# Attention and two expert layers on one core: the projections of q and k as plain f32 in two 64-row halves, and the last tokens as one tile

## The chip, the cores and the metric

The kernel runs on one core of one Trainium2 chip. The metric is the device time of one launch in microseconds (us), as the median of three runs. Two executions agree within 0.2%, about 1.7 us here.

## What is computed

Three stages follow each other. The first is an attention with random features, the second a dense layer with a leaky rectifier, the third a layer of 8 experts of which each token uses one. The change touches the first stage alone.

```python
# B=4 batches, H=8 heads, S=576 tokens, D=64; omega: (M=128, 64)
def phi(x):                                   # x: (B, H, S, 64), scaled by 64**-0.25
    h = einsum('bhsd,md->bhsm', x, omega) - sum(x*x)/2
    return exp(h - max(h)) / sqrt(128)
q_p, k_p = phi(q_s), phi(k_s)
kv = einsum('bhsm,bhsd->bhmd', k_p, v);  z = sum(k_p, tokens)
x  = (q_p @ kv) / (q_p @ z + 1e-6)            # -> (2304, 512)
h  = x @ w_in;  x2 = max(0.01*h, h) @ w_out   # w_in (512, 2048), w_out (2048, 512)
...                                           # 8 experts, top 1, on x2
```

## The kernel before

Heads are worked in 16 **pairs** (two heads of one batch, 128 columns together). Of a head's 576 tokens, 512 are four blocks of 128 and the **last 64** are kept apart: those of both heads of a pair, for q and for k, form one tile "m". Per pair the steps are, by their names in the table `STEPS`: loads `Lk Lq Lm Lv`; squares, halving and sums `s a r` (sums of x*x); transposes on TensorE `Tk Tq Tm` (L520); copies of the transposed tile to SBUF as a high part `xh` and a low part `xl` (L314, L323), both f32r; projections `Pk0 Pk1 Pq0 Pq1 Pm` (L541 to L543), each 128-token block by three matmuls of 256 columns (high by high, high by low, low by high) against a block-diagonal `om_hi` and `om_lo`, so that one matmul gives two token blocks of a head (for "m", q and k); maxima `m` (L551); biases `b c` (L564, or L571 and L572 on GpSimd); exponentials `e` on ScalarE (L583); `KVm KV0 KV1` (L590, L595), plain f32 matmuls of q's and k's features; transposes `F0 F1 Fm` of q's features (L614, L610) and their copies `fc`; numerators `U0 U1` (L629, L634); denominators `dn` (L650 to L654); ratios `xs0 xs1` (L661, L668), where the last tokens are scaled head by head in two instructions of 64 rows; transposes `XT Xm` (L674, L678); and the copies into the dense layer's input `xb` as high and low parts, `yh yl` and, again head by head for the last tokens, `yhm ylm`.

Beside the pairs run two other streams in the same stretch. Ten **conversions** (`RW C0 C1 CX C2 CH CL`, L396 to L421) make f32r high and low parts of the dense weights. And **dense steps** of the first group of 5 weight chunks (45 steps of 256 tokens by one chunk): `M1` (12 matmuls, L750 to L752), `HS GG GH GL` on ScalarE, VectorE and GpSimd, `M2` (6 matmuls of 512 columns in two banks, L791 to L793, 3 for each 128 tokens). A dense step can begin when its tokens' pairs are through `yl` and `ylm`, so 4 pairs of a batch at least.

The order of all these steps on every engine is made before the launch by `issue_order` (L152). It takes the durations of `STEPS` (L52) for each engine on which a step may run ("P" TensorE, "V" VectorE, "A" ScalarE, "G" GpSimd, "D" the DMA queue), ranks written into the table, and the 8 PSUM banks ("+tk" takes a bank, "-tk" gives it back), and puts down step, engine and banks. The kernel issues the steps in that order; an engine works strictly in it. What dense steps are left when the last pair is through (L1361) runs behind it, then the groups of 3 and 8 chunks, then the experts.

Of the kernel before, what the change touches and what calls it, by code (L numbers as in the profile page):

```python
# [9 lines left out]
F32 = mybir.dt.float32  # L10
# [57 lines left out]
    "xlk": ("p", (("V", 0.6, 291.1),), "-tk", "xhk"),  # L68
    "Tm": ("p", (("P", 0.11, -1226.3),), "+tm", "Lm"),
    "xhm": ("p", (("A", 0.158, -513.9), ("V", 0.2, 157.5)), "", "Tm Pm-1"),  # L70
    "xlm": ("p", (("V", 0.2, -1168.8),), "-tm", "xhm"),
    "Tq": ("p", (("P", 0.44, -203.4),), "+tq", "Lq"),
    "xhq": ("p", (("A", 0.47, 1466.0), ("V", 0.6, 259.7)), "", "Tq Pq0-1 Pq1-1"),
    "xlq": ("p", (("V", 0.6, -1992.3),), "-tq", "xhq"),
# [1512 lines left out]
```

## Time and profile before

| | us |
|---|---|
| median of 3 runs (872.69 to 873.39) | 873.34 |
| profiled execution, its own time | 875.46 |
| its span in the trace | 873.4 |
| PE busy / DVE busy in the span | 812.6 / 564.1 |

The span is one execution on the hardware. A PE matmul is pipelined: its row's length holds the way through the array, so matmuls overlap in the rows, and what one costs is the distance to the next one's start. An f32 matmul that is no transpose stands in the trace as two instructions, so the four matmuls of one `KV` step are 8 rows.

### The profile page before, as it was taken

Reading aid. Unit: us, or ns where it says so; the run is one execution under the profiler, and the core shown is the slowest. Engines: PE = TensorE matmul, PEld = TensorE weight load, DVE = VectorE, ACT = ScalarE, POOL = GpSimd, SP = SyncE. Lnnn points to the kernel's source line nnn. Section 1 sums busy time; section 2 is a strip of 40 time slices with the busy share of each in tenths; the row PEclk is TensorE's granted clock in tenths of the full one; section 3 lists DMA queues with packets and bytes.
Section 4 is the critical chain, followed back from the end, with each engine's and each line's share of the span. In section 5 each row is a group of like instructions: output and inputs, shape, how many; then the busy total and the mean of one; then the engine's idle time right before and its main releaser. Section 6 shows DMA issues by size and latency. Waiting matters only on the chain. (4 is left out here: it accounts for less than half of the span.)

```text
span 873.4 us, 14417 instructions
## 1 busy us (share of the span) xinstructions
PE 812.6 (93%) x5018; PEld 727.9 (83%) x5018; DVE 564.1 (65%) x1406; ACT 354.4 (41%) x898; POOL 293.4 (34%) x384
## 2 busy tenths in 40 slices
PE   8988898999999999999999999898888799999993
PEld 8877788899998899999998988786677689987892
DVE  7999999688755627625487988979888222222121
ACT  6776656266536534423333332444432111112110
POOL 6323435121004435424424244444655211111000
PEclk9999979999999999999999999989999899999997
DMA  6433423122117415645112331467561211111100
GB/s 183 125 99 88 125 68 91 49 58 52 39 36 234 142 53 180 228 157 175 44 61 36 50 38 36 110 181 120 98 76 59 62 38 50 50 49 38 36 25 29
DMA packets 68309, 75.73 MB, mean 87 GB/s; under 512 B 32691, under 2 KB 49148, under 8 KB 68094
## 3 DMA queue, kind: packets, MB, share of 16 engines
q1 hardware_dynamic: 64766, 65.19, 28.6%
q0 software_dynamic: 3456, 9.49, 3.5%
q8 instruction: 42, 0.69, 0.4%
q14 instruction: 45, 0.37, 0.2%
HBM read 55.65 MB, written 19.00 MB: 85 GB/s over the span
## 5 line engine op out<-in xcount | busy, mean ns | idle before, releaser
L323 POOL TENSOR_TENSOR glo<-gg,ghi 128x384 fp32r<-128x384 f32 (+1 forms) x93 | 97.6, 1050 | 213.6 <-ACT ghi L314 179.8
L750 PE MATMUL ph<-xb,ring 128*128 128x384 f32 (+1 forms) x444 | 141.4, 319 | 1.3 <-ACT hs L314 0.6
L752 PE MATMUL ph<-xb,ring 128*128 128x384 f32 (+1 forms) x444 | 141.0, 318 | 0.0
L751 PE MATMUL ph<-xb,ring 128*128 128x384 f32 (+1 forms) x444 | 140.3, 316 | 0.0
L760 DVE SCALAR_TENSOR_TENSOR gg<-hs 128x384 f32<-128x384 f32 (+1 forms) x111 | 67.9, 612 | 84.8 <-ACT hs L314 79.7
L925 DVE CUSTOM_DVE_ANT_0 jv<-xl,en 128x512 bf16<-128x512 f32 x144 | 121.2, 865 | 1.4
L791 PE MATMUL px<-ring,ghi 128*128 128x512 f32 x288 | 114.7, 398 | 5.8 <-ACT ghi L314 5.8
L793 PE MATMUL px<-ring,glo 128*128 128x512 f32 x288 | 113.1, 398 | 2.4 <-POOL glo L323 2.4
L792 PE MATMUL px<-ring,ghi 128*128 128x512 f32 x288 | 114.2, 396 | 0.6 <-DVE ring L323 0.6
L750 PEld LDWEIGHTS ph<-xb,ring 128*128 128x128 f32 x444 | 84.4, 190 | 7.1 <-ACT hs L314 1.4
L314 ACT CAST ghi<-gg 128x384 fp32r<-128x384 f32 (+1 forms) x93 | 44.8, 482 | 109.9 <-DVE gg L760 109.8
L751 PEld LDWEIGHTS ph<-xb,ring 128*128 128x128 f32 x444 | 84.4, 190 | 4.0
L752 PEld LDWEIGHTS ph<-xb,ring 128*128 128x128 f32 x444 | 84.5, 190 | 0.3
L314 ACT COPY hs<-ph 128x384 f32<-128x384 f32 (+1 forms) x109 | 47.3, 434 | 86.5 <-PE ph L752 84.4
L1203 DVE SCALAR_TENSOR_TENSOR fh<-fh,fh 128x256 fp32r<-128x256 f32 x48 | 20.4, 425 | 91.0 <-ACT fh L1202 91.0
L793 PEld LDWEIGHTS px<-ring,glo 128*128 128x128 f32 x288 | 54.0, 189 | 16.6 <-POOL glo L323 5.1
L791 PEld LDWEIGHTS px<-ring,ghi 128*128 128x128 f32 x288 | 54.7, 190 | 14.9 <-ACT ghi L314 7.0
L1202 ACT ACTIVATE fh<-fh 128x256 fp32r<-128x256 f32 x48 | 18.5, 386 | 112.7 <-PE fh L1196 112.6
L792 PEld LDWEIGHTS px<-ring,ghi 128*128 128x128 f32 x288 | 54.6, 190 | 9.0 <-DVE ring L323 0.9
L1269 POOL DMA_INDIRECT out_dram<-ot,xg x14 | 14.1, 1008 | 123.6 <-DVE ot L1268 79.4
L1194 PE MATMUL fh<-xth,w 128*128 128x256 f32 x128 | 35.8, 282 | 0.0
L1195 PE MATMUL fh<-xth,w 128*128 128x256 f32 x128 | 35.8, 281 | 0.0
(1272 smaller groups left out, 1958.3 us busy)
## 6 DMA issues: line engine op xcount, KB each, us to landing
xl<-xpart SPq DMA_DIRECT2D x36, 256.0 KB
rawi<-in_moe_w_in_dram SPq DMA_DIRECT2D x16, 512.0 KB
rawo<-in_moe_w_out_dram SPq DMA_DIRECT2D x16, 512.0 KB
rws<-in_moe_w_dram SPq DMA_DIRECT2D x16, 512.0 KB
xpart<-xo SPq DMA_DIRECT2D x18, 256.0 KB
xpart<-xl SPq DMA_DIRECT2D x18, 256.0 KB
xs<-xl SPq DMA_DIRECT2D x18, 256.0 KB
k<-in_k_dram SPq DMA_DIRECT2D x16, 256.0 KB
```

Source lines behind the costliest of these rows:

```text
L314: (A.copy if e == "A" else ENG[e].tensor_copy)(out_, in_)
L323: eng.tensor_tensor(lo, src, hi.bitcast(F32), op=ALU.subtract)
L750: PE.matmul(ph, wh, xb[blk][:, 0, kk, d], start=(kk == 0), stop=False)
L751: PE.matmul(ph, wl, xb[blk][:, 0, kk, d], start=False, stop=False)
L752: PE.matmul(ph, wh, xb[blk][:, 1, kk, d], start=False, stop=(kk == 3))
L760: V.scalar_tensor_tensor(gs["gg"], gs["hs"], 0.01, gs["hs"], op0=ALU.mult, op1=ALU.max)
L791: PE.matmul(px, ghi[:, d], r[:, 2, :], start=first, stop=False)
L792: PE.matmul(px, ghi[:, d], r[:, 3, :], start=False, stop=False)
L793: PE.matmul(px, glo[:, d], r[:, 2, :], start=False, stop=last)
L925: V.tensor_tensor_reduce(out=jv, in0=xfin[t], in1=rt["en"][:, e, :], scale=1.0, scalar=0.0, op0=ALU.mult, op1=ALU.add, accum_out=lg[:, j, ...
L1194: PE.matmul(ph, wh, xh, start=(kk == 0), stop=False)
L1195: PE.matmul(ph, wl, xh, start=False, stop=False)
```

## The change

The projections of the 512-token part take plain f32 operands. The copy of the transposed tile is one step, `xk xq xm` (L314 in the changed kernel's helper), with no low part. `Pk` and `Pq` are one step each, of 8 matmuls: for each of the 4 blocks of the transposed tile, whose rows 0 to 63 are an even token block of a head and rows 64 to 127 the odd one, one matmul with the upper and one with the lower 64 rows, each against its half of `om_bd`, into two different banks ("++pk" takes two). `Pm` is one f32 matmul of 256 columns. What stood by head in `KV`, `U`, `mk0/mk1` and `xs` now stands by token parity. The denominators are 10 columns wide: the last tokens of both heads are added, inverted and masked together (`own`), scaled by one instruction into `xm`, and moved by an ordinary f32 matmul against `two` (the sum of both halves of the identity) to 128 rows by 64 columns, so that `yhm` and `ylm` are one instruction each instead of two.

```diff
-    "xhk": ("p", (("A", 0.47, -769.1), ("V", 0.6, 1084.7)), "", "Tk Pk0-1 Pk1-1"),
-    "xlk": ("p", (("V", 0.6, 291.1),), "-tk", "xhk"),
-    "Pk0": ("p", (("P", 0.69, -189.8),), "+pk0", "xlk"),
+    "xk": ("p", (("A", 0.47, 462.5), ("V", 0.6, -718.0)), "-tk", "Tk Pk-2"),
+    "Pk": ("p", (("P", 1.4, -292.1),), "++pk", "xk"),
...
-                late = t + dur if x == e and e != "D" else end + 0.15 * (e == "V" and x == "G")
+                late = t + dur if x == e == "P" else end + 0.15 * (e == "V" and x == "G")
...
-            PE.matmul(o, hi, om_hi, start=True, stop=False)
-            PE.matmul(o, hi, om_lo, start=False, stop=False)
-            PE.matmul(o, lo, om_hi, start=False, stop=True)
+        ps = [bank(f"pj{i}{x}{j}") for j in range(2)]
+        xT = st[i].pop("x" + x)
+        for u in range(4):
+            for j in range(2):
+                r = slice(j * D, (j + 1) * D)
+                PE.matmul(
+                    ps[j][:, u * M : (u + 1) * M], xT[r, u * P : (u + 1) * P],
+                    om_bd[r, j * M : (j + 1) * M], start=True, stop=True,
+                )
+    def proj_last(i):
+        ps = st[i]["pm"] = bank(f"pj{i}m")
+        PE.matmul(ps[:, 0 : 2 * M], st[i].pop("xm"), om_bd, start=True, stop=True)
...
-        for h in range(2):
-            r, _, d = m_view(i, h)
-            V.tensor_scalar_add(dn[r, 8:9], d, 1e-6)
+        V.tensor_scalar_add(dn[:, 0:4], u_view(i, 0)[:, :, D], 1e-6)
+        V.tensor_scalar_add(dn[:, 4:10], u_view(i, 1)[:, :, D], 1e-6)
         V.reciprocal(dn, dn)
+        V.tensor_tensor(dn[:, 8:10], dn[:, 8:10], own, op=ALU.mult)
...
-            for j in range(2):
-                r, u, _ = m_view(i, j)
-                V.tensor_scalar_mul(xms[i % 2][r, j * D : (j + 1) * D], u, dn[r, 8:9])
+            V.tensor_tensor(
+                xms[i % 2].rearrange("p (h d) -> p h d", h=2), u_view(i, 1)[:, 4:6, 0:D],
+                dn[:, 8:10].unsqueeze(2).to_broadcast([P, 2, D]), op=ALU.mult,
+            )
...
-        PE.transpose(ps[:, 0:P], xms[i % 2], ident)
+        PE.matmul(ps[:, 0:D], xms[i % 2], two, start=True, stop=True)
```

The table's ranks are all new, so the whole order of the first stretch is new. On VectorE, before, from the denominators of pair 2 (`dn`) to the copies of its last tokens (`xpm` to `xb`):

```order
L650 TENSOR_SCALAR dn_136<-u_0_841 128x4
L650 TENSOR_SCALAR dn_136<-u_1_853 128x4
L653 TENSOR_SCALAR dn_136<-u_1_853 64x1 x2
L654 RECIPROCAL dn_136<-dn_136 128x9
L661 TENSOR_TENSOR xt_910<-u_0_841,dn_136 128x4x64
L314 COPY qT_919<-pq_887 128x512
L661 TENSOR_TENSOR xt_910<-u_1_853,dn_136 128x4x64
L668 TENSOR_SCALAR xm_138<-u_1_853,dn_136 64x64 x2
L323 TENSOR_TENSOR xl4q<-tr4q,xh4q 128x512
L323 TENSOR_TENSOR xl4m<-tr4m,xh4m 128x128
L314 CAST xb_131<-xpm_942 64x64 x2
L323 TENSOR_TENSOR xb_131<-xpm_942,xb_131 64x64 x2
```

Now, the same place (pair 2 again):

```order
L652 TENSOR_SCALAR dn_132<-u_0_743 128x4
L653 TENSOR_SCALAR dn_132<-u_1_790 128x6
L654 RECIPROCAL dn_132<-dn_132 128x10
L655 TENSOR_TENSOR dn_132<-dn_132,own 128x2
L320 TENSOR_TENSOR xb_127<-xpm_807,xb_127 128x64
L662 TENSOR_TENSOR xt_832<-u_0_743,dn_132 128x2x2x64
L662 TENSOR_TENSOR xt_832<-u_1_790,dn_132 128x2x2x64
L669 TENSOR_TENSOR xm_134<-u_1_790,dn_132 128x128
L566 SCALAR_TENSOR_TENSOR mx4k_788<-ss_728,mx4k_788 128x4x2
L509 TENSOR_REDUCE ss_728<-sqs4m 128x2
L549 TENSOR_REDUCE mx4m<-pj4m 128x2
L509 TENSOR_REDUCE ss_728<-sqs4q 128x8
```

The ratios of the last tokens (`xm`) are one row of 128 columns where they were two of 64 rows, their low part in `xb` is one row where it was two, a mask row has come to the denominators, and no low parts `xl4q` and `xl4m` follow. On TensorE, before, the last-token projection of pair 4 with the work around it (`pq` is the transpose of q's features, `xp` and `xpm` that of the ratios, `tr` that of the inputs, `kv` the `KV` steps):

```order
L614 MATMUL pq_935<-ident,f3q_902 128x128 x4
L678 MATMUL xpm_942<-ident,xm_138 128x128
L674 MATMUL xp_944<-ident,xt_910 128x128 x4
L520 MATMUL tr5k<-ident,k_711 128x128 x4
L541 MATMUL pj4m<-om_hi,xh4m 128x256
L542 MATMUL pj4m<-om_lo,xh4m 128x256
L543 MATMUL pj4m<-om_hi,xl4m 128x256
L590 MATMUL kv_973<-v1s_135,f3m 128x130
L595 MATMUL kv_973<-v1s_135,f3k_801 128x65 x4
L595 MATMUL kv_973<-v1s_135,f3k_825 128x65 x4
L541 MATMUL pj4q_994<-om_hi,xh4q 128x256
```

Now, around the last-token projection of pair 6:

```order
L532 MATMUL pj6k_1089<-om_bd,x6k 128x128
L532 MATMUL pj6k_1090<-om_bd,x6k 128x128
L594 MATMUL kv_1118<-v1s_131,f5m 128x130
L601 MATMUL kv_1118<-v1s_131,f5k_1021 128x65 x4
L678 MATMUL xp_1137<-ident,xt_1120 128x128 x4
L516 MATMUL tr6m<-ident,m_979 128x128
L682 MATMUL xpm_1149<-two,xm_135 128x64
L620 MATMUL pq_1154<-ident,f4q_1128 128x128 x4
L516 MATMUL tr6q<-ident,q_1005 128x128 x4
L542 MATMUL pj6m<-om_bd,x6m 128x256
L620 MATMUL pq_1180<-ident,f4q_1113 128x128 x4
```

The three projection rows of a last-token tile are one, the projections of a pair stand in one block of 8 with the two banks in turn, and the last tokens' ratios go through a matmul against `two`. On TensorE the projections of q and k stand in 28 such blocks between other work, for 32 steps. Further on in TensorE's order, 4 `M1` steps stand ahead of `XT` of pair 8 before, and 14 now; ahead of `XT` of pair 15 it is 22 and 25.

## Rows read from the trace of the kernel before

**Rows 1.** The page: span, busy time, busy tenths of DVE in 40 slices

```profile
span 873.4 us, 14417 instructions
...
PE 812.6 (93%) x5018; PEld 727.9 (83%) x5018; DVE 564.1 (65%) x1406; ACT 354.4 (41%) x898; POOL 293.4 (34%) x384
...
DVE  7999999688755627625487988979888222222121
```

**Rows 2.** Stretches: length, busy PE, PEld, DVE, ACT, POOL (count), PE clock, DMA

```profile
0.00:150.00 150.00, 133.13 (x980) 119.76 (x981) 139.19 (x377) 99.80 (x302) 60.63 (x144) 0.95 0.40 111
120.00:130.00 10.00, 8.37 (x44) 7.38 (x44) 9.26 (x28) 5.72 (x18) 3.81 (x6) 0.66 0.32 92
150.00:256.00 106.00, 104.35 (x808) 98.85 (x809) 80.07 (x241) 55.54 (x168) 15.60 (x23) 1.00 0.16 44
256.00:873.00 617.00, 575.11 (x3233) 509.29 (x3231) 344.82 (x791) 199.03 (x430) 217.14 (x217) 0.98 0.34 88
```

**Rows 3.** PE in order of time: start, length, line, operation, out<-in, form, count

```profile
149.56 0.28 PE L543 MATMUL pj10q<-om_hi,xl10q 128*128 128x256 f32 x1
149.89 0.39 PE L750 MATMUL ph<-xb,ring 128*128 128x256 f32 x1
...
254.86 0.27 PE L678 MATMUL xpm<-ident,xm 128*128 128x128 f32 x1
254.97 0.60 PE L674 MATMUL xp<-ident,xt 128*128 128x128 f32 x4
...
256.10 0.40 PE L791 MATMUL px<-ring,ghi 128*128 128x512 f32 x1
256.34 0.39 PE L792 MATMUL px<-ring,ghi 128*128 128x512 f32 x1
```

**Rows 4.** DVE in order of time, behind the turn; last: idle and releaser

```profile
161.12 0.43 DVE L760 SCALAR_TENSOR_TENSOR gg<-hs 128x256 f32<-128x256 f32 x1 [0.85 <-ACT hs L314]
```

**Rows 5.** PE in order of time: f32 halves, then a projection of pair 5

```profile
65.57 1.90 PE L595 MATMUL kv<-v1s,f4k 128*128 128x65 f32 x16
67.28 0.36 PE L541 MATMUL pj5q<-om_hi,xh5q 128*128 128x256 f32 x1
67.48 0.28 PE L542 MATMUL pj5q<-om_lo,xh5q 128*128 128x256 f32 x1
67.59 0.28 PE L543 MATMUL pj5q<-om_hi,xl5q 128*128 128x256 f32 x1
```

**Rows 6.** DVE in order of time: the steps that the change touches

```profile
62.79 0.57 DVE L668 TENSOR_SCALAR xm<-u,dn 64x64 f32<-64x64 f32 x2
63.40 0.29 DVE L323 TENSOR_TENSOR xl5m<-tr5m,xh5m 128x128 fp32r<-128x128 f32 x1
63.60 0.68 DVE L551 TENSOR_REDUCE mx5k<-pj5k 128x4 f32<-128x512 f32 x1
64.20 0.47 DVE L314 CAST xb<-xpm 64x64 fp32r<-64x64 f32 x2
64.70 0.48 DVE L323 TENSOR_TENSOR xb<-xpm,xb 64x64 fp32r<-64x64 f32 x2
65.20 0.69 DVE L323 TENSOR_TENSOR xl5q<-tr5q,xh5q 128x512 fp32r<-128x512 f32 x1
65.81 0.41 DVE L551 TENSOR_REDUCE mx5m<-pj5m 128x2 f32<-128x256 f32 x1
```

**Rows 7.** DVE in order of time: one conversion twice, and denominators

```profile
46.91 0.41 DVE L396 TENSOR_SCALAR tti<-rawi 128x512 int32<-128x512 int32 x1
...
138.78 0.95 DVE L396 TENSOR_SCALAR tti<-rawi 128x512 int32<-128x512 int32 x1
...
140.38 0.22 DVE L650 TENSOR_SCALAR dn<-u 128x4 f32<-128x4 f32 x2
...
141.12 0.76 DVE L661 TENSOR_TENSOR xt<-u,dn 128x256 f32<-128x256 f32 x2
```

**Rows 8.** One line (the numerators): weight loads, min, median and max ns

```profile
L629 PEld LDWEIGHTS u<-kvf,qT x256: 186/192/245, 20.5 to 250.4; 128*128 128x128 f32 x128
```

More of the change, by code (lines that the diff above doesn't have):

```diff
@@ L170, in issue_order @@
             if name[0] == "P":
-                need.add(("ol", 0))
+                need.add(("oh", 0))
             if name == "M1":
@@ L208, in issue_order @@
         spots = {}
-        for b, among in (("+h", (0, 1)), ("+x", (2, 3, 4, 5, 6)), ("+", range(8))):
-            n = 2 if b == "+x" else 1
+        for b, among in (("+h", (0, 1)), ("+x", (2, 3, 4, 5, 6)), ("+", range(8)), ("++", range(8))):
+            n = 2 if b in ("+x", "++") else 1
             got = sorted((rooms[r] + 0.05, r) for r in among if r in rooms)[:n]
@@ L230, in issue_order @@
         if kind_of_room(s):
-            t = max(t, spots.get(b, spots["+"])[0])
-            got = spots[b][1] if b in spots else (
-                max(r for r in rooms if rooms[r] + 0.05 <= t),)
+            t = max(t, spot(b)[0])
+            got = spots[b][1] if b in spots else tuple(
+                sorted(r for r in rooms if rooms[r] + 0.05 <= t)[-len(spot(b)[1]) :])
             for r in got:
                 del rooms[r]
-            held[b[1:], i] = list(got)
+            held[b.lstrip("+"), i] = list(got)
         for x, _, _ in modes:
@@ L253, in issue_order @@
         if b[:1] == "-":
-            rooms[held[b[1:], i - NRING + 1 if b == "-x" else i][name == "XV"]] = end
+            rooms[held[b[1:], i - NRING + 1 if b == "-x" else i][name in ("XV", "ek1", "eq1")]] = end
         for u in users.get(s, ()):
             for x in AHEAD:
-                late = t + dur if x == e and e != "D" else end + 0.15 * (e == "V" and x == "G")
+                late = t + dur if x == e == "P" else end + 0.15 * (e == "V" and x == "G")
                 ready[u][x] = max(ready[u][x], late)
@@ L339, in tile_attention_moe_moe, with om_step @@
         PE.matmul(warm[:, 0:P], wz, wz, start=True, stop=True)
-    om_hi = atp.tile([P, 2 * M], F32R, name="om_hi", tag="om_hi")
-    om_lo = atp.tile([P, 2 * M], F32R, name="om_lo", tag="om_lo")
-    obd = atp.tile([P, 2 * M], F32, name="obd", tag="xt", bufs=2)
-    V.memset(obd, 0.0)
-    A.copy(om_hi, obd)
-    V.tensor_copy(om_lo, obd)
+    om_bd = atp.tile([P, 2 * M], F32, name="om_bd", tag="om_bd")
+    V.memset(om_bd, 0.0)
     oms = {}
-    def om_step(name):
+    def om_step(name, e):
         if name == "om":
@@ L435, in tile_attention_moe_moe @@
     v1s = [atp.tile([P, 5, 2, D + 2], F32, name=f"v1s{j}", tag=f"v1{j}") for j in range(2)]
-    dns = [atp.tile([P, 9], F32, name=f"dn{j}", tag=f"dn{j}") for j in range(2)]
+    dns = [atp.tile([P, 10], F32, name=f"dn{j}", tag=f"dn{j}") for j in range(2)]
     xms = [atp.tile([P, P], F32, name=f"xm{j}", tag=f"xm{j}") for j in range(2)]
@@ L443, in tile_attention_moe_moe @@
             G.memset(v1s[j][h * 64 : h * 64 + 64, 4, h, D : D + 1], 1.0)
-        G.memset(xms[j], 0.0)
+    own = atp.tile([P, 2], F32, name="own", tag="own")
+    G.memset(own, 0.0)
+    for h in range(2):
+        G.memset(own[h * 64 : h * 64 + 64, h : h + 1], 1.0)
+    two = atp.tile([P, D], F32, name="two", tag="two")
+    G.tensor_tensor(two, ident[:, 0:D], ident[:, D:P], op=ALU.add)
     def part(i):
@@ L521, in trans, with trans_copy, proj @@
         st[i]["t" + p] = ps[:, :w]
-    def trans_hi(i, e, p):
-        ps = st[i]["t" + p]
-        st[i]["xh" + p] = hi = atp.tile([P, ps.shape[1]], F32R, name=f"xh{i}{p}", tag=f"xh{p}")
-        copy(e, hi, ps)
-    def trans_lo(i, p):
-        ps = st[i].pop("t" + p)
-        st[i]["xl" + p] = lo = atp.tile([P, ps.shape[1]], F32R, name=f"xl{i}{p}", tag=f"xl{p}")
-        split_lo(V, lo, ps, st[i]["xh" + p])
-    def proj(i, p):
-        x, n, u0 = (p[0], 2, 2 * int(p[1]) * P) if p != "m" else ("m", 1, 0)
-        ps = bank(f"pj{i}{p}")
-        for j in range(n):
-            u = slice(u0 + j * P, u0 + (j + 1) * P)
-            hi, lo = st[i]["xh" + x][:, u], st[i]["xl" + x][:, u]
-            o = ps[:, j * 256 : (j + 1) * 256]
-            PE.matmul(o, hi, om_hi, start=True, stop=False)
-            PE.matmul(o, hi, om_lo, start=False, stop=False)
-            PE.matmul(o, lo, om_hi, start=False, stop=True)
-        st[i]["p" + p] = ps
+    def trans_copy(i, e, p):
+        ps = st[i].pop("t" + p)
+        st[i]["x" + p] = x = atp.tile([P, ps.shape[1]], F32, name=f"x{i}{p}", tag=f"x{p}", bufs=2)
+        copy(e, x, ps)
+    def proj(i, x):
+        ps = [bank(f"pj{i}{x}{j}") for j in range(2)]
[7 more added lines that the diff above has]
+                )
+        for j in range(2):
+            st[i][f"p{x}{j}"] = ps[j]
+    def proj_last(i):
+        ps = st[i]["pm"] = bank(f"pj{i}m")
+        PE.matmul(ps[:, 0 : 2 * M], st[i].pop("xm"), om_bd, start=True, stop=True)
     def largest(i, p):
@@ L562, in bias @@
         mx = st[i]["b" + x][:, : 2 * (r.stop - r.start)]
+        if x != "m":
+            mx = mx.rearrange("p (b h a) -> p h a b", b=2, h=2)
+            sv = sv.rearrange("p (h a b) -> p h a b", h=2, b=2)
         if e == "V":
@@ L570, in bias @@
             t = t[:, : 2 * (r.stop - r.start)]
+            if x != "m":
+                t = t.rearrange("p (h a b) -> p h a b", h=2, b=2)
             G.tensor_scalar_mul(t, sv, half)
@@ L590, in kv_last, with kv @@
         PE.matmul(pk, st[i]["fm"][:, 1, :], vs[i][:, 4, :, 0 : D + 1], start=True, stop=False)
-    def kv(i, h):
-        f = st[i].pop(f"fk{h}")
-        for t in range(4):
-            PE.matmul(
-                st[i]["kv"][:, h, :], f[:, t, :], vs[i][:, t, h, 0 : D + 1],
-                start=False, stop=(t == 3 and "kv_" in st[i]),
-            )
-        st[i]["kv_"] = h
+    def kv(i, j):
+        f = st[i].pop(f"fk{j}")
+        for h in range(2):
+            for a in range(2):
+                PE.matmul(
+                    st[i]["kv"][:, h, :], f[:, 2 * h + a, :], vs[i][:, 2 * a + j, h, 0 : D + 1],
+                    start=False, stop=(h == 1 and a == 1 and "kv_" in st[i]),
+                )
+        st[i]["kv_"] = j
     def kv_copy(i, e):
@@ L621, in f_copy, with numer @@
         copy(e, t, ps[:, 0:w])
-    def numer(i, h):
-        ps = st[i][f"u{h}"] = bank(f"u{i}_{h}")
-        qT, kvf = st[i].pop(f"qT{h}"), st[i]["kvf"]
-        for t in range(4):
+    def numer(i, j):
+        ps = st[i][f"u{j}"] = bank(f"u{i}_{j}")
+        qT, kvf = st[i].pop(f"qT{j}"), st[i]["kvf"]
+        for g in range(4):
             PE.matmul(
-                ps[:, t * (D + 1) : (t + 1) * (D + 1)], qT[:, t * P : (t + 1) * P],
-                kvf[:, h, :], start=True, stop=True,
+                ps[:, g * (D + 1) : (g + 1) * (D + 1)], qT[:, g * P : (g + 1) * P],
+                kvf[:, g // 2, :], start=True, stop=True,
             )
-        if h == 1:
+        if j == 1:
             PE.matmul(
@@ L637, in numer, with u_view, ratio @@
             )
-    def u_view(i, h):
-        return st[i][f"u{h}"][:, 0 : 4 * (D + 1)].rearrange("p (t d) -> p t d", t=4)
-    def m_view(i, h):
-        r, c = slice(h * 64, h * 64 + 64), (4 + h) * (D + 1)
-        return r, st[i]["u1"][r, c : c + D], st[i]["u1"][r, c + D : c + D + 1]
+    def u_view(i, j):
+        w = 6 if j else 4
+        return st[i][f"u{j}"][:, 0 : w * (D + 1)].rearrange("p (g d) -> p g d", g=w)
     def dens(i):
         dn = dns[i % 2]
-        for h in range(2):
-            V.tensor_scalar_add(dn[:, 4 * h : 4 * h + 4], u_view(i, h)[:, :, D], 1e-6)
-        for h in range(2):
-            r, _, d = m_view(i, h)
-            V.tensor_scalar_add(dn[r, 8:9], d, 1e-6)
+        V.tensor_scalar_add(dn[:, 0:4], u_view(i, 0)[:, :, D], 1e-6)
+        V.tensor_scalar_add(dn[:, 4:10], u_view(i, 1)[:, :, D], 1e-6)
         V.reciprocal(dn, dn)
-    def ratio(i, h):
+        V.tensor_tensor(dn[:, 8:10], dn[:, 8:10], own, op=ALU.mult)
+    def ratio(i, j):
         if "xt" not in st[i]:
@@ L688, in x_parts @@
             w = min(XB - off, end - t0)
-            if m:
-                for h in range(2):
-                    r = slice(h * 64, h * 64 + 64)
-                    yield st[i]["xpm"][r, h * 64 : h * 64 + 64], [
-                        xb[blk][r, j, hp, off : off + w] for j in range(2)
-                    ]
-            else:
-                yield st[i]["xp"][:, t0 - b * S : t0 - b * S + w], [
-                    xb[blk][:, j, hp, off : off + w] for j in range(2)
-                ]
+            at = 0 if m else t0 - b * S
+            yield st[i]["xpm" if m else "xp"][:, at : at + w], [
+                xb[blk][:, j, hp, off : off + w] for j in range(2)
+            ]
             t0 += w
@@ L1328, in tile_attention_moe_moe @@
             if kind == "o":
[L1329 removed]
+                om_step(name, e)
             elif kind == "p":
```

34 lines of the change are left out of this document (15 added, 19 removed), and 153 rows, old and new, of the table STEPS.

## Prediction

> **What bounds the kernel now.** I read the page first, then stretches of the span, then the two engines in order of time. On the page PE is busy for 93% of the span, DVE for 65%, and the tenths of DVE are high only at the front and in the routing far behind [rows 1]. The stretches split the change's part in two [rows 2]. From 0 to 150 us DVE is busy for 139.2 of 150 us, PE at a mean clock of 0.95; from 120 to 130 us PE starts only 44 matmuls and the clock is 0.66. From 150 to 256 us PE is busy for 104.4 of 106 us at full clock, and DVE falls to 80.1. So DVE ends last in the first part and PE in the second. The turn is seen in time: a projection of pair 10 starts at 149.56, and at 149.89 a run of dense steps begins [rows 3], after which DVE's dense work waits for ScalarE and so for PE [rows 4]. The last pair's transposes are at 254.86 and 254.97 [rows 3]. What follows, 617 us, is the same work in both kernels, except that it begins with as many dense steps fewer as the first stretch took in.
>
> PE's busy share hides what it lost, since a row holds the way through the array: a dense matmul of 256 columns is 0.28 long and the next starts 0.12 later, a 512-column one 0.23 later, and one f32 half-instruction of the `KV` step costs (67.28 - 65.57)/16 = 0.107 [rows 3, 5]. The 980 matmuls up to 150 us [rows 2], less 35 for warming up, come to 114 us at such distances (0.12 on the mean). **PE lost about 35.5 us before 149.9 and nearly nothing from there to 256.** That is all that a lighter DVE can win.
>
> How the 35.5 come about can be counted from the order. I added, step by step, what DVE and PE are handed, with durations from distances of starts in the trace. DVE's sum runs ahead of PE's by at most 29.4 us, 144.3 against 115.0, just where the run of dense steps begins. With 6.1 us of start-up that is the 35.5. The count and the trace agree, so I use the same count for the changed order.
>
> **The change, part by part.** *DVE.* A pair loses the low parts of q, k and m: 0.61 + 0.61 + 0.20 (65.20 to 65.81, 63.40 to 63.60 [rows 6]), 1.42 us. The last tokens' ratios go from two rows (62.79 to 63.40, 0.61) to one, about 0.30; their low part from 0.50 (64.70 to 65.20) to 0.22, and their high part likewise where DVE has it, 11 pairs before and 8 after [rows 6]. The denominators go from five rows in 0.74 us (140.38 to 141.12) [rows 7] to four that depend on each other; I keep 0.74. Over 16 pairs this takes off 16 x (1.42 + 0.31 + 0.28) + 11 x 0.50 - 8 x 0.22 = 36 us. The new order gives DVE more of some steps (copies of q, k and m 17 instead of 3, halvings 17 instead of 3, feature copies 10 instead of 6, five more dense steps: some 17 us) and fewer of others (biases 48 instead of 78, high parts of dense steps 6 instead of 18, low parts of conversions 2 instead of 5: some 17 us). DVE's sum up to the end of the pairs is 186 us with 26 dense steps, against 222 with 21.
>
> *PE.* A projection of a tile was 12 matmuls 0.12 apart, 1.43 us. Now it is 8 f32 matmuls of 64 rows and 128 columns, so 16 half-instructions. No row shows a split array. Bounds: 16 x 0.107 = 1.7 us if the halves take turns like whole ones [rows 5], 0.86 if two always run side by side. A change between whole and split array may besides leave it to run empty: by rows, what a matmul's length has over the distance, 0.28 - 0.12 = 0.16 us [rows 5], at both ends of the 28 blocks of projections, 56 x 0.16 = 9.0 us, 0.28 for each of the 32 projections. I take 1.4: the middle, 1.29, and half of that, because no row tells the cases apart. Whole range: 0.86 to 2.0. The last-token projection goes from 3 x 0.12 = 0.36 to one f32 matmul of 256 columns; two halves of 0.107 (as 65 columns cost) would be 0.21, two as long as a 512-column matmul's distance (0.23) 0.46; I take 0.43, near the upper end, as the columns go through twice; the lower end is worth 3.5 us over the pairs. `Xm` goes from one transpose, 0.11 (254.86 to 254.97 [rows 3]), to an f32 matmul of two halves, 0.21 to 0.22. Sum: 32 x (1.4 - 1.43) + 16 x (0.07 + 0.11) = +2.0 us. Bounds: -15.3 at 0.86, +11.5 at 1.7, +20.5 with the array emptied as well.
>
> A rule of the Trainium skill speaks against the split: its page "TensorEngine Tiling (Array Packing)", section "Key Properties", says that changing the tiling mode drains TensorE. No row here shows such a change. By that rule all of the 9.0 us would fall due, 4.5 more than I count, and the forecast would be 863.
>
> *ScalarE and GpSimd.* ScalarE makes the copies that DVE does not (23 instead of 30 of q and k), and 20 high parts of dense steps instead of 3; it was busy for 99.8 of 150 us and has room. GpSimd gets some 15 us more and was busy for 60.6 [rows 2]. What hides them is that neither ends last; a late bias can hold ScalarE's exponentials, which is part of the slack below. No DMA is added, and no queue gets a new wait.
>
> *Banks.* `Pk` and `Pq` now hold two of the 8 banks each from the first matmul to the last exponential, before one after the other. That can hold a transpose or an `M1`; I have no row for it and count it into the slack.
>
> *The order.* The same count on the new order, with 1.4 for a projection: DVE's lead peaks at 5.7 us (71.6 against 65.9, in a conversion beside pair 6), and from there PE's sum is the larger, because 14 dense steps instead of 4 stand ahead of the transposes of pair 8. With both engines handed about the same, waits of one step for another show that a lead covered before. In the trace, 25.3 us were lost between 40 and 150 us while the lead grew by some 17; 8 us, clock included, are such slack. I add 7 us.
>
> **Sum.** Lead 5.7 - 29.4 = -23.7; slack +7; PE's own work +2.0: -14.7 us. Against the profiled execution, 875.5, that is 860.8; against the median 873.3, which lies 2.1 below, **858.6**.
>
> **The rivals.**
>
> *Halves side by side.* If both halves of the array work at once throughout, a projection costs 0.86: PE's work falls by 15.3, DVE's lead peaks at 13 us, since PE gets faster too: 13 - 29.4 + 7 - 15.3 = -24.7, 848.6. For it: the two halves use different rows and banks. Against: each matmul also needs its weights, and a load's row is 192 ns [rows 8], longer than the distance. By the Trainium skill's page "TensorEngine Tiling (Array Packing)", section "Theoretical Speedup", a contraction of at most 64 gains up to 2x, which is this case; no row here shows it.
>
> *Halves in turn.* At 1.7 the lead nearly vanishes (2.1), PE's work grows by 11.5: 2.1 - 29.4 + 7 + 11.5 = -8.8, 864.5. With 9.0 more from an array that empties 56 times, lead 0.7: -1.2, 872.1.
>
> *Slower: weight loads exposed.* If a half's weights can't be loaded while the other half or the earlier matmul runs, a half-instruction takes at least its load's 0.192 [rows 8] and a projection 16 x 0.192 = 3.1. PE's work grows by 56 us, the lead is gone: 0.7 - 29.4 + 7 + 56 = +34, 908. It turns slower than before from about 2.0 us for a projection, 0.125 for a half. Against it: in whole-array f32 matmuls the load is hidden, 192 ns long at a distance of 107 [rows 5, 8].
>
> *DVE keeps the lead.* The same conversion took 0.41 us in one place and 0.95 in another [rows 7]. If GpSimd's extra work stretches these and the new strided operands cost DVE too, some 7 us of the lead come back: 866.
>
> **How the numbers follow.** Forecast (a projection at 1.2 to 1.6, slack 2 to 12): 0.50, its own range 850 to 868. Halves side by side, 849: 0.17. Halves in turn, 864 to 874: 0.18, about a quarter of it within 0.2% of before. DVE keeps the lead, 866: 0.07. Slower, 880 to 908: 0.08. A measurement tells 0.2% (1.7 us) from nothing. Faster: 0.50 + 0.17 + 0.13 + 0.07 = 0.87; same 0.05; slower 0.08. The range takes in the fast rival and most of the halves in turn and leaves out the slower case: 847 to 871.
>
> **What would show it.** In the changed trace: the projections' rows, 8 x 2 of them, 1.4 us from the first start to the next step's; DVE's busy share below 0.9 between 60 and 150 us; PE's clock 1.0 from 100 to 150; dense steps from about 70 us on and PE nearly without gaps from about 100; the last pair's transposes at about 250 us with 25 dense steps ahead instead of 22. It is wrong if the projections take 2 us or more, if PE waits for DVE until 150 us as before, or if the stretch after the pairs changes its pace.

## The result and the profile after

The changed kernel takes **843.49 us**, median of 4 runs (841.22 to 844.17), against 873.37 us for the kernel before on the same chip (872.69 to 874.35). The ratio is 0.9653 with a 95% interval of 0.9632 to 0.9673. The gain is 29.9 us, twice the forecast 14.7, and the time lies below the forecast range of 847 to 871. The direction was right, the size was not. The profiled execution of the changed kernel took 841.22 us, 2.3 below the median, and that of before 875.46, 2.1 above it, so the two traces differ by 4.4 us more than the medians do.

The page of the changed kernel, for [rows 1]: the span, the busy times and VectorE's tenths in 40 slices of 21 us.

```profile
span 839.3 us, 14540 instructions
...
PE 793.4 (95%) x5146; PEld 711.1 (85%) x5146; DVE 521.6 (62%) x1282; ACT 343.5 (41%) x880; POOL 305.3 (36%) x442
...
DVE  7999966776646577345679798988894222222121
```

VectorE's run of nines now has 4 slices (some 21 to 105 us), where it had 6 (22 to 153 us); it lost 42.5 us of busy time. Its stretches, for [rows 2]: length, busy time of PE, PEld, DVE, ACT and POOL, then the granted clock of PE and the DMA share.

```profile
0.00:100.00 100.00, 93.14 (x822) 83.14 (x823) 91.44 (x237) 68.62 (x209) 61.82 (x162) 1.00 0.55 152
120.00:130.00 10.00, 10.00 (x83) 9.06 (x83) 7.30 (x23) 7.01 (x23) 0.45 (x2) 1.00 0.40 101
150.00:233.00 83.00, 83.00 (x738) 77.78 (x735) 55.83 (x166) 50.88 (x162) 15.40 (x34) 1.00 0.15 42
233.00:291.90 58.90, 58.90 (x372) 53.01 (x371) 31.34 (x55) 31.98 (x79) 24.01 (x28) 1.00 0.47 157
```

The last stretch before the second group of weight chunks, in the kernel before:

```profile
256.00:325.80 69.80, 68.66 (x427) 60.39 (x426) 35.11 (x61) 35.48 (x88) 28.54 (x33) 1.00 0.42 139
```

From 120 to 130 us PE starts 83 matmuls at full clock, where it started 44 at 0.66 [rows 2]. Up to 100 us VectorE is still busy for 91% and PE has 6.9 us without a matmul; from there to the second group, at 291.9 us, PE shows no gap at all. Before, PE still had 1.65 us without a matmul from 150 to 256 us [rows 2] and 1.14 from 256 to 325.8, 2.8 us together.

TensorE in order of time, for [rows 3]: start, length, line, operation, form, count. These are, in the changed kernel, the last pair's transposes and the first matmul of 384 columns, with which the second group begins.

```profile
231.72 0.60 PE L678 MATMUL xp<-ident,xt 128*128 128x128 f32 x4
232.16 0.33 PE L682 MATMUL xpm<-two,xm 128*128 128x64 f32 x2
...
291.89 0.33 PE L749 MATMUL ph<-xb,ring 128*128 128x384 f32 x1
```

And the same first matmul of 384 columns in the kernel before:

```profile
325.81 0.33 PE L750 MATMUL ph<-xb,ring 128*128 128x384 f32 x1
```

It starts 33.9 us earlier. What follows it takes 547.4 us of the span, against 547.6 before. **The whole gain lies in the first stage and in the first group of dense steps**, as the prediction had assumed.

The projections in the changed kernel, where [rows 5] had the old ones: one row is one block of 16 half-instructions.

```profile
27.27 1.16 PE L532 MATMUL pj3k<-om_bd,x3k 64*128 64x128 f32 x16
28.26 1.06 PE L532 MATMUL pj2q<-om_bd,x2q 64*128 64x128 f32 x16
29.25 0.49 PE L594 MATMUL kv<-v1s,f2m 128*128 128x130 f32 x2
...
107.33 1.16 PE L532 MATMUL pj8k<-om_bd,x8k 64*128 64x128 f32 x16
108.42 1.11 PE L635 MATMUL u<-kvf,qT 128*128 128x65 f32 x8
...
120.46 0.40 PE L792 MATMUL px<-ring,glo 128*128 128x512 f32 x1
120.79 1.16 PE L532 MATMUL pj9k<-om_bd,x9k 64*128 64x128 f32 x16
121.88 0.66 PE L516 MATMUL tr10k<-ident,k 128*128 128x128 f32 x4
```

The reader is to look at distances of starts. Two blocks behind each other take 1.98 us (27.27 to 29.25), one alone 1.09 (107.33 to 108.42). The second of two adds 0.89, and this is what a projection costs without its edges: 0.056 us for each of the 16 half-instructions, where one of the whole array costs 0.107 [rows 5]. The other 0.20 of a block alone are edges, and there are edges outside it: a 512-column matmul just ahead of one gives way after 0.33 instead of 0.23, and the step behind it is longer by 0.06 (`tr10k`) to 0.11 (`u`) than where whole rows precede it (the run with whole rows below). So **a projection costs 0.89, and the change to half rows and back some 0.37 for each block**: 0.20 inside, 0.10 ahead, 0.06 to 0.11 behind.

VectorE behind the denominators of pair 5 (the sixth mask row in order of time), for [rows 6]:

```profile
91.37 0.16 DVE L655 TENSOR_TENSOR dn<-dn,own 128x2 f32<-128x2 f32 x1
...
92.43 0.28 DVE L669 TENSOR_TENSOR xm<-u,dn 128x128 f32<-128x128 f32 x1
...
95.29 0.22 DVE L320 TENSOR_TENSOR xb<-xpm,xb 128x64 fp32r<-128x64 f32 x1
```

The ratios of the last tokens are one row of 0.28 and their low part one of 0.22, as the prediction had them (0.30 and 0.22).

### The profile page after: what moved, and what is told of

Its sections match the earlier page's. It is cut to its first block, busy times and chain, and to the rows that moved or that the text cites. A ratio compares the mean times of both kernels' runs of the same rounds, so it can differ in the third digit from the quotient of the medians.

```text
span 839.3 us, 14540 instructions
## 1 busy us (share of the span) xinstructions
PE 793.4 (95%) x5146; PEld 711.1 (85%) x5146; DVE 521.6 (62%) x1282; ACT 343.5 (41%) x880; POOL 305.3 (36%) x442
## 5 line engine op out<-in xcount | busy, mean ns | idle before, releaser
L759 DVE SCALAR_TENSOR_TENSOR gg<-hs 128x384 f32<-128x384 f32 (+1 forms) x111 | 65.2, 587 | 80.7 <-ACT hs L311 77.1
L311 ACT CAST ghi<-gg 128x384 fp32r<-128x384 f32 (+1 forms) x105 | 49.7, 473 | 112.2 <-DVE gg L759 106.3
L311 ACT COPY hs<-ph 128x384 f32<-128x384 f32 (+1 forms) x103 | 44.9, 436 | 74.9 <-PE ph L751 74.6
```

What stands on the lines that cost most here:

```text
L311: (A.copy if e == "A" else ENG[e].tensor_copy)(out_, in_)
L759: V.scalar_tensor_tensor(gs["gg"], gs["hs"], 0.01, gs["hs"], op0=ALU.mult, op1=ALU.max)
```

## The experiments

The theory after this result, A below: up to about 107 us VectorE ends last, from there on TensorE; what counts is VectorE's lead over TensorE and then TensorE's own work, and the split projection makes both ends cheaper. Its rivals were that the order written anew brings the gain, or that the projection's halves bring nothing. Four groups of runs follow. The medians of before beside them were 872.9 to 874.5 us.

### What the two halves are worth

**Whole rows.** The changed kernel with each projection's matmul on all 128 rows: the number of matmuls and their columns stay as they are, and since `om_bd` is zero in the other block, so does what is computed.

```diff
-                r = slice(j * D, (j + 1) * D)
...
-                    ps[j][:, u * M : (u + 1) * M], xT[r, u * P : (u + 1) * P],
-                    om_bd[r, j * M : (j + 1) * M], start=True, stop=True,
+                    ps[j][:, u * M : (u + 1) * M], xT[:, u * P : (u + 1) * P],
+                    om_bd[:, j * M : (j + 1) * M], start=True, stop=True,
```

> The changed kernel with one edit: each of the 8 f32 matmuls of a projection takes all 128 rows of the array instead of 64, against the same zero-padded columns of om_bd, so that banks, order and instruction count stay. Theory A (the two halves run side by side, which the forecast priced too high at 1.4 us a projection; in the changed trace 1.1): without the split a projection costs 16 x 0.107 = 1.7 us, PE's work grows by 32 x 0.61 = 19.5 us, DVE's lead falls from 9.7 to 1.9 by the count over the order: +11.7 us on the changed kernel, about 855. Rival B (the short distance of 0.06 us has nothing to do with the halves; an f32 matmul of 128 columns simply costs that): no change, 843. Rival C (the lead is not what PE waits for): the whole 19.5 us, 863.

Measured: 856.83 us (854.99 to 858.83), ratio to before 0.9797 [0.9768, 0.9827]. So the halves are worth 13.3 us; A had 11.7. In this run's trace, the same projections of pairs 8 and 9 as above, the second with what stands around it, and the last one:

```profile
110.09 1.95 PE L532 MATMUL pj8k<-om_bd,x8k 128*128 128x128 f32 x16
...
124.40 0.39 PE L792 MATMUL px<-ring,glo 128*128 128x512 f32 x1
124.63 1.95 PE L532 MATMUL pj9k<-om_bd,x9k 128*128 128x128 f32 x16
126.41 0.60 PE L516 MATMUL tr10k<-ident,k 128*128 128x128 f32 x4
...
230.84 2.00 PE L532 MATMUL pj15q<-om_bd,x15q 128*128 128x128 f32 x16
```

The last projection with halves, in the changed kernel:

```profile
218.44 1.16 PE L532 MATMUL pj15q<-om_bd,x15q 64*128 64x128 f32 x16
```

A block is 1.78 (126.41 - 124.63), where it is 0.89 in halves without its edges: half. With whole rows there are no edges: the 512-column matmul ahead gives way after 0.23, and `tr10k` behind is 0.60 long, not 0.66. With them a block alone saves some 0.5 to 0.6 us and two behind each other some 1.4, 19 us for the 28 blocks, of which 13.3 arrive. The order of steps is the same in both kernels, so the blocks can be followed one by one. The projection of pair 8 starts at 110.09 with whole rows and at 107.33 with halves: the 15 projections ahead of it, some 0.6 us cheaper each, brought only 2.8 us together, 0.2 each. From there to the last one, 230.84 and 218.44, the stretches with 16 projections are 120.8 and 111.1 us long: 0.6 each. **While VectorE ends last, a cheaper projection is mostly waited away; behind 107 us it counts nearly in full.**

**The same half in a row.** The changed kernel with its two loops exchanged, so that neighbouring matmuls of a block name the same half.

```diff
-        for u in range(4):
-            for j in range(2):
+        for j in range(2):
+            for u in range(4):
```

> The changed kernel with the two loops of a projection exchanged: the four multiplies of one 64-row half come one after another, then the four of the other half; the same sixteen instructions, only in another order. Theory A (the halves are cheap because neighbouring instructions name different halves and run beside each other): in a row on the same half an instruction costs what a whole-row one does, 0.107 us a start, a projection 16 x 0.107 = 1.7 us, and the kernel ends where the one with whole rows ended, about 857 us. Theory B (a contraction of 64 rows is itself cheaper, whatever stands next to it): starts stay near 0.06 us and the time at 843 us.

Measured: 852.43 us (851.50 to 853.23), ratio 0.9765 [0.9734, 0.9795]. It is 8.9 us slower than with halves in turn and 4.4 faster than whole rows, so nearer to A, which had 857. TensorE, where the projections of pair 3 (k) and 2 (q) meet, and then that of pair 8:

```profile
29.08 0.27 PE L532 MATMUL pj3k<-om_bd,x3k 64*128 64x128 f32 x1
29.18 0.27 PE L532 MATMUL pj2q<-om_bd,x2q 64*128 64x128 f32 x1
29.19 0.27 PE L532 MATMUL pj3k<-om_bd,x3k 64*128 64x128 f32 x1
29.30 0.27 PE L532 MATMUL pj2q<-om_bd,x2q 64*128 64x128 f32 x1
...
108.22 1.71 PE L532 MATMUL pj8k<-om_bd,x8k 64*128 64x128 f32 x16
109.86 0.32 PE L635 MATMUL u<-kvf,qT 128*128 128x65 f32 x1
```

Here the two halves are seen working at once: `pj3k` finishes its lower half at starts 0.11 apart (29.08, 29.19) while `pj2q` goes on in the upper half at its own 0.11 (29.18, 29.30). A half alone costs what the whole array costs; the gain is that a neighbour in the other half runs beside it. A block alone takes 1.64 us (109.86 - 108.22), since its own two halves meet only where one ends and the other begins. With the edges ahead and behind (0.10 and 0.06 to 0.11) that is no gain on the 1.78 to 1.84 of whole rows. The gain comes from the four places where two blocks meet, some 0.7 us each, 2.9 of the 4.4; the rest isn't located. Theory B, that 64 rows are cheaper by themselves, is out.

### What each part of the change is worth in the old order

**The last tokens as one tile, alone.** Before's table and order; the denominators, ratios, `Xm` and `yhm`, `ylm` as in the changed kernel.

```diff
-                V.tensor_scalar_mul(xms[i % 2][r, j * D : (j + 1) * D], u, dn[r, 8:9])
+                xms[i % 2].rearrange("p (h d) -> p h d", h=2), u_view(i, 1)[:, 4:6, 0:D],
+                dn[:, 8:10].unsqueeze(2).to_broadcast([P, 2, D]), op=ALU.mult,
...
-        PE.transpose(ps[:, 0:P], xms[i % 2], ident)
+        PE.matmul(ps[:, 0:D], xms[i % 2], two, start=True, stop=True)
```

> The kernel before, its table and order untouched, with the last-token part of the change alone: denominators 10 columns wide with the mask, one scaling row, the matmul against two, one row instead of two for the copies into xb. Theory A: DVE's lead peaks at 22.0 instead of 29.4 us, PE's own work grows by 16 x 0.11 = 1.8: -5.6 us on the kernel before, about 868. Rival B (small rows on DVE cost nothing that ends last): within 1.7 us of 873.

**Plain f32, alone.** Before's table and order; no low parts, and each block of a projection one f32 matmul of whole rows and 256 columns.

```diff
-            PE.matmul(o, hi, om_hi, start=True, stop=False)
-            PE.matmul(o, hi, om_lo, start=False, stop=False)
-            PE.matmul(o, lo, om_hi, start=False, stop=True)
+            PE.matmul(o, hi, om_hi, start=True, stop=True)
```

> The kernel before, its table and order untouched, with plain f32 projections and no low parts, but with whole rows: each 128-token block is one f32 matmul of 256 columns instead of three f32r ones, the steps xl and ol issue nothing. Theory A: DVE's lead peaks at 5.9 instead of 29.4 us; PE's own work grows by 64 x (0.86 - 0.715) + 16 x 0.07 = 10.5: -13.0 us on the kernel before, about 860. Rival B (the lead counts for less in the old order, whose dense steps stand late): -5 or less, 868 and more. Rival C (PE's work is hidden as well, since PE had gaps): -23, 850.

**Both, in the old order.** The edits of the last two together.

> The kernel before, its table of steps and their order untouched, with both of the parts that were tried alone: no low parts and plain f32 projections on whole rows, and the last tokens of both heads as one tile. Beside the changed kernel with whole rows (856.8 us), which does the same work in the new order, it tells what the new order brings. Theory A (the order brings nothing, the work taken from DVE and PE's own work set the time): the two alone took 10.5 and 10.4 us; together DVE's lead over PE is gone, 29.4 to 0.6 us, against 12.3 us more of PE work: 873.4 - 28.8 + 12.3 = 857 us, granted clock 1.00 up to 150 us. Theory B (the order written anew carries a good part of the gain): 862 us or more.

Measured: the last tokens alone 862.97 us (861.09 to 864.61), ratio 0.9874 [0.9847, 0.9901]; plain f32 alone 863.02 (862.12 to 863.79), 0.9875 [0.9853, 0.9897]; both 858.84 (855.55 to 861.62), 0.9832 [0.9789, 0.9874]. Plain f32 brought 10.4 of the 13 that A had. The last tokens brought 10.5, more than either theory had (5.6 and at most 1.7). Both together lie nearer to A's 857 than to B's 862, with a granted clock of 1.00 up to 150 us. The stretch of 100 to 150 us shows where part of the gain is; first before, then the last tokens alone, then plain f32 alone:

```profile
100.00:150.00 50.00, 43.32 (x294) 39.43 (x293) 47.22 (x122) 31.07 (x96) 22.97 (x26) 0.86 0.32 90
```

```profile
100.00:150.00 50.00, 44.17 (x314) 40.78 (x313) 46.53 (x114) 31.02 (x90) 23.60 (x26) 0.93 0.31 89
```

```profile
100.00:150.00 50.00, 45.48 (x309) 40.35 (x310) 46.45 (x117) 31.67 (x94) 22.91 (x26) 1.00 0.32 94
```

When VectorE is lighter the granted clock of this stretch rises from 0.86 to 0.93 with the last tokens alone and to 1.00 with plain f32 alone, 3.5 and 7.0 us of full clock. With the last tokens alone the waits behind 150 us, 2.8 us before, are nearly gone as well, up to the second group:

```profile
150.00:312.60 162.60, 162.38 (x1180) 151.88 (x1179) 99.70 (x254) 86.38 (x242) 39.82 (x52) 1.00 0.26 85
```

Neither stands in A's count; these are rows of one execution each. The parts don't add up: 10.4 + 10.5 = 20.9, both together 14.7. A reading of this, which no run tries by itself, is that either takes the same waits away, and that behind them stands TensorE's longer plain f32 work. Both in the old order (858.8) and the same work in the new one (whole rows, 856.8) have intervals that overlap: that the new order brings something of its own isn't shown.

### Where VectorE's time counts

**Low parts again.** The changed kernel with the low part of each transposed tile computed again on VectorE, and used by nobody; first for all pairs, then for pairs 8 to 15 alone, then for 0 to 7 alone (with `if i >= 8:` or `if i < 8:` ahead).

```diff
         copy(e, x, ps)
+        lo = atp.tile([P, 512], F32R, name=f"xl{i}{p}", tag="xl")
+        split_lo(V, lo[:, : ps.shape[1]], ps, x)
```

> The changed kernel with the work of the low parts put back on DVE: behind each copy of a transposed tile DVE subtracts it from the bank into a tile that nobody reads (0.61, 0.61 and 0.20 us a pair), as it did before. The order of all else stays. Theory A (PE's loss in the first stretch is DVE's lead in handed-out work plus the start, with no further slack): DVE's lead peaks at 23.4 instead of 9.7 us, +13.7 us on the changed kernel, about 857. Rival B (the new order, not the lighter DVE, brought the gain): within 3 us of 843. Rival C (all of 16 x 1.42 us come back): +22.7, 866.

> The changed kernel, with the unused low part of each transposed tile (one VectorE subtraction for q, k and m, 1.42 us a pair) made again for pairs 8 to 15 alone, 11.4 us of VectorE's time. Made for all 16 pairs it cost 23.8 us. Theory A (VectorE ends last only up to about 107 us, where the projections of pair 8 begin; behind it TensorE ends last and VectorE has room): 843 to 846 us. Theory B (the subtraction delays every projection, wherever it stands, since the bank and the copy wait for it): half of the 23.8 us, 855 us.

> The other half: the unused low parts for pairs 0 to 7 alone, 11.4 us of VectorE's time in the stretch where it ends last. Theory A: the 11.4 us come out in full, and what the granted clock takes when TensorE waits more often comes on top, 855 to 866 us, most of the 23.8 us. Theory B: as many as the other half, 855 us. Which part is the clock is read from the granted clock of 0 to 110 us: with all 16 it was 0.90 up to 100 us, which is 10 us of waiting at full clock.

Measured: all pairs 867.25 us (861.87 to 867.77), ratio 0.9901 [0.9864, 0.9939], 23.8 above the changed kernel; pairs 8 to 15 850.92 (850.52 to 851.64), 0.9734 [0.9718, 0.9750], 7.4 above; pairs 0 to 7 855.39 (854.71 to 856.43), 0.9782 [0.9765, 0.9798], 11.9 above. For all pairs the number is rival C's (866), not A's (857). The early half costs more than the late one, but its 855 was the number of both theories. The late half is far from free: 850.9 lies between A's 846 and B's 855, nearer to B. The waits of VectorE in that run, from 100 to 230 us (tile and line, what it waited for, us in total, times, longest), show two of its single waits:

```profile
DVE xl9q L320 <- ACT x9q L311: 2.0, 1, 2.0
DVE xl11q L320 <- ACT x11q L311: 1.7, 1, 1.7
```

There the high part is ScalarE's copy, and VectorE, which works strictly in order, stands still until it is made. So this edit adds a wait besides the work, and TensorE's bank is kept longer; it isn't a clean price of VectorE's time, and of theory B something holds. These runs don't confirm A's sizes. With all pairs the granted clock falls as well; the stretches of that run, then one of the run with pairs 0 to 7:

```profile
20.00:30.00 10.00, 7.38 (x66) 6.71 (x65) 9.86 (x27) 4.77 (x15) 4.36 (x6) 0.99 0.66 180
30.00:40.00 10.00, 9.88 (x77) 8.66 (x78) 8.60 (x19) 6.62 (x23) 4.28 (x16) 0.67 0.22 62
...
0.00:100.00 100.00, 88.72 (x694) 78.12 (x694) 87.69 (x224) 58.17 (x174) 51.26 (x148) 0.90 0.46 132
```

```profile
0.00:50.00 50.00, 43.07 (x357) 37.66 (x357) 42.39 (x108) 28.71 (x86) 25.91 (x98) 0.90 0.52 144
50.00:100.00 50.00, 44.22 (x366) 38.08 (x365) 48.73 (x122) 32.47 (x99) 29.05 (x56) 1.00 0.44 126
```

After a stretch in which PE was busy for 7.38 of 10 us the clock is 0.67 in the next. At 0.90 over 100 us, 10 us are lost beside the waits; the changed kernel has 1.00 there. That is the size of what A's 857 lacks. With pairs 0 to 7 the clock costs 5 us (0.90 over 50 us) and PE is without a matmul for 12.7 us up to 100, 5.9 more than in the changed kernel: 10.9 of the 11.9 us. So only some half of the 11.4 us of VectorE's time came out as waits; the clock is the other half. This is read from these rows; no run held the clock up with the waits left in.

**The mask on GpSimd.** In the changed kernel the masking of the last tokens' denominators took 0.16 us in some pairs and up to 1.03 in others. Moved to GpSimd:

```diff
-        V.tensor_tensor(dn[:, 8:10], dn[:, 8:10], own, op=ALU.mult)
+        G.tensor_tensor(dn[:, 8:10], dn[:, 8:10], own, op=ALU.mult)
```

> The changed kernel with the masking of the two last-token denominators (one 128x2 multiply per pair) issued on GpSimd instead of VectorE. In the changed kernel's trace this multiply takes 0.16 us where GpSimd is idle or in its own short steps and 0.63 to 1.03 us in four of the first six pairs. Theory A (VectorE's lead in the first 100 us still costs the time that it is long): up to 2.7 us of the lead goes, 840 to 842 us. Theory B (the tile of last tokens then waits for GpSimd's queue, whose steps are of 1 us and more): VectorE stands still at the next multiply and the time is 845 us or more.

Measured: 843.18 us (840.63 to 844.60), ratio 0.9657 [0.9620, 0.9694]: no difference from the changed kernel, and neither theory. VectorE is busy for 3 us less up to 100 us, but in the profiled execution PE lost as much otherwise (the clock was 0.97 in the first 50 us, and one transpose waited 1.5 us for its load). Inconclusive.

### What the order is worth

**The projection booked otherwise.** The table books `Pk` and `Pq` at 1.4; in these four runs at 1.1, 1.25, 1.5 and 1.7. The instructions are the same, their order shifts.

```diff
-    "Pk": ("p", (("P", 1.4, -292.1),), "++pk", "xk"),
+    "Pk": ("p", (("P", 1.1, -292.1),), "++pk", "xk"),
...
-    "Pq": ("p", (("P", 1.4, 1306.1),), "++pq", "xq"),
+    "Pq": ("p", (("P", 1.1, 1306.1),), "++pq", "xq"),
```

> The changed kernel with one number of its table changed, the length at which a projection of q or k is booked: 1.1 instead of 1.4. The instructions are the same, their order shifts. Theory A (by 100 us PE never waits any more, and of what it loses before, most is the start): the time stays within 3 us of 843. Theory B (the order is late because projections end earlier than booked): the rest of DVE's lead, up to 9 us, shrinks, 836 to 840 us.

> The changed kernel with a projection booked at 1.25 in the table, between the 1.4 of the changed kernel and the 1.1 that took 851.0 us. Theory A (what an order brings depends on how its steps happen to fall around 100 us, not on the number): anywhere from 841 to 853 us, no trend. Theory B (a longer booking is steadily better, since it leaves TensorE work in hand): between the two, 846 to 849 us.

> The changed kernel with a projection booked at 1.5 in the table (1.4 in the changed kernel; measured 1.09 from its first start to the next step's). At 1.25 it took 849.1 us and at 1.1 851.0. Theory A (which steps fall next to each other, not the number, decides): 841 to 853 us, later than 843.5 as likely by luck as 1.25 and 1.1 were. Theory B (a longer booking is steadily better): below 843 us.

> The same with 1.7. Theory A: 841 to 853 us, on either side of the result at 1.5. Theory B: below the result at 1.5, 842 us or less.

| booked | median, us | range | ratio, 95% |
|---|---|---|---|
| 1.1 | 851.00 | 849.94 to 851.53 | 0.9745 [0.9715, 0.9775] |
| 1.25 | 849.07 | 848.43 to 849.29 | 0.9711 [0.9695, 0.9727] |
| 1.4 (the change) | 843.49 | 841.22 to 844.17 | 0.9653 [0.9632, 0.9673] |
| 1.5 | 843.50 | 842.89 to 846.09 | 0.9659 [0.9632, 0.9686] |
| 1.7 | 846.02 | 844.87 to 847.15 | 0.9690 [0.9661, 0.9719] |

The number that is nearest to the 1.09 from a block's first start to the next step's gives the latest of the five, against both theories of the first of these runs; there is no steady trend either, since 1.7 isn't better than 1.5, so theory B of the later runs is out. Theory A is left, but with 841 to 853 us it could hardly miss. None beats the changed kernel; 1.5 and 1.7 have intervals that overlap its own. TensorE in the run at 1.1, between 106 and 111 us:

```profile
106.06 1.08 PE L635 MATMUL u<-kvf,qT 128*128 128x65 f32 x8
108.69 0.39 PE L749 MATMUL ph<-xb,ring 128*128 128x256 f32 x1 [1.56 <-ACT hs L311]
...
109.92 0.42 PE L751 MATMUL ph<-xb,ring 128*128 128x256 f32 x1
110.13 0.41 PE L749 MATMUL ph<-xb,ring 128*128 128x256 f32 x1
```

and its stretches there, then the changed kernel's:

```profile
100.00:120.00 20.00, 16.82 (x110) 14.72 (x108) 14.95 (x37) 9.88 (x30) 8.91 (x16) 0.91 0.20 61
110.00:120.00 10.00, 9.58 (x60) 8.70 (x60) 6.34 (x18) 2.90 (x8) 3.48 (x6) 0.85 0.14 52
```

```profile
100.00:120.00 20.00, 20.00 (x157) 18.16 (x156) 14.41 (x38) 9.38 (x28) 9.17 (x18) 1.00 0.15 44
```

The changed kernel has dense steps at hand here and starts 157 matmuls in 20 us; the order at 1.1 has spent them, waits, and then the dense matmuls come 0.21 apart instead of 0.12: half the clock, the lower of its two levels (1.2 and 2.4 GHz). The waits (3.2 us) and the clock (0.09 x 20 = 1.8 us) make some 5 of the 7.5 us; the rest isn't located.

## Why the prediction missed

**What held.** The place of the gain, the turn from VectorE to TensorE, VectorE's steps and their durations, and the rest of the span unchanged. Of the signs at the prediction's end, PE's clock is 1.0 in the slices from 100 to 150 us, dense steps run from 65 us and PE has no gaps from 100. VectorE falls below 0.9 only at 90 us, not at 60; the projection takes 1.09 from its first start to the next step's instead of 1.4, and the last transposes come at 231.7 instead of about 250.

**The term that failed first: PE's own work, +2.0.** The projection was taken at 1.4, between the halves side by side (0.86) and in turn (1.7), "because no row tells the cases apart". Its halves, taken at 1.29, cost 0.89: they run side by side throughout, at 0.056 a start against the bound's 0.86/16 = 0.054. By the Trainium skill, "TensorEngine Tiling (Array Packing)", section "Theoretical Speedup", a contraction of at most 64 gains up to 2 times; the runs show 1.78/0.89 = 2.0 within a block, and only with the halves in turn. The change of mode was mis-sized the other way. I counted half of 9.0 us for it, and 28 blocks at 0.37 come to 10.4. By the same page of the Trainium skill, section "Key Properties", changing the tiling mode drains TensorE; the trace agrees, with these 10.4 us beside the 9.0 that the prediction had worked out by that rule. So the projections come to 32 x 0.89 + 10.4 = 38.9 us against 32 x 1.43 = 45.8, 1.22 for one instead of 1.4. With `Pm` as forecast and `Xm` at 0.14 (232.16 to the next start at 232.30) instead of 0.21 or 0.22, PE's own work changes by -6.9 + 16 x (0.07 + 0.03) = -5.3 instead of +2.0: 7.3 of the missing 15.2 us. The old price holds to about 1 us. In [rows 5] an old block's second matmul starts 0.20 behind the first instead of 0.12, but the first starts early, 0.03 behind a transpose where 0.11 is the rule:

```profile
59.52 0.27 PE L520 MATMUL tr5m<-ident,m 128*128 128x128 f32 x1
59.55 0.36 PE L541 MATMUL pj5k<-om_hi,xh5k 128*128 128x256 f32 x1
59.75 0.28 PE L542 MATMUL pj5k<-om_lo,xh5k 128*128 128x256 f32 x1
```

**The second: slack, +7.** I added 7 us for waits of one step for another, from the kernel before, in which 25.3 us were lost while the lead grew by 17. In the changed kernel the time that PE loses up to the second group, counted by distances, is 12 to 16 us, as the edges of the blocks are counted with the work or not. That is 6.1 of start-up and the lead (below), with no slack left; this is an estimate, not a measurement. Part of those 8 us was the clock, as the prediction says ("clock included"): it was 0.86 from 100 to 150 us, and it is 1.00 now. That price went away with the waits; the prediction kept it.

**The third, against it: the lead, 5.7.** With about 1.1 for a projection the same count gives 9.7 us (88.4 against 78.7, at the low parts of pair 5), since PE gets faster too; at 1.22 it is some 8, between the two counts. The rival with the halves side by side had seen this.

**A term put at nothing.** The prediction let PE lose "nearly nothing" from the turn to 256 us, and went no further. PE was without a matmul for 2.8 us from 150 us to the second group, and in the changed kernel for none.

So 8 - 29.4 = -21.4 for the lead, no slack, -5.3 for PE and -2.8 behind the turn come to -29.5; measured -29.9. The terms carry no such accuracy: the lead is an estimate, and the order has a share of its own (see the range).

**The rivals.** "Halves side by side" (0.17) had the mechanism. That it came within 5 us is in part luck: it had no price for the edges (10 us), and against that stand the slack of 7 that it kept and a lead of 13 instead of 8. "Halves in turn" and "weight loads exposed" are out by the rows: starts lie 0.056 apart, less than the 0.192 of a load [rows 8], so the loads run beside other work. "DVE keeps the lead" did not happen, though a step of VectorE can be longer beside GpSimd's work (the mask, below).

**The range.** It ended at the fast rival's 847 with its slack in, and left out that two terms, slack and price, could fall on the same side. Besides, the four other bookings show what the prediction had no term for: the same instructions in five orders took 843 to 851 us, a gain of 22 to 30. So up to 7.5 of the 15.2 us that the prediction missed can be the luck of this order, and the share of each term above is open by as much.

## What to carry over

Price a part of the chip that the trace doesn't show by its bounds, but ask what neighbouring instructions name: matmuls on alternating 64-row halves cost 0.056 here, in a row on the same half 0.11. Price the change of mode besides: some 0.37 us for each block of them. Take work from the engine that ends last and count its lead before adding slack; waits that were paid partly in clock vanish with the waits. A change that writes the order anew is known only to the spread of such orders, in the five tried here 8 of 843 us.

## What the hardware showed beyond that

The two halves of the array can hold two different projections at once: with the same half in a row, the second's first half ran beside the first's second half, each at its own 0.11. A multiply of 128 by 2 elements on VectorE took 0.16 us in eleven pairs and 0.63 to 1.03 in five of the same kernel. One of the five, and what GpSimd did there:

```profile
43.36 1.27 POOL L320 TENSOR_TENSOR ring<-tti,ring 128x512 fp32r<-128x512 f32 x1 [0.22 <-ACT ring L311]
...
43.91 0.73 DVE L655 TENSOR_TENSOR dn<-dn,own 128x2 f32<-128x2 f32 x1
```

The multiply ends at 44.64, GpSimd's step at 44.63. In all five a GpSimd step of 0.73 us or more had begun just before, and the multiply's row ends with it, to 0.02 us; in none of the eleven had such a step begun. That GpSimd's step holds VectorE's row fits this, but was not tried by itself.
